# First k products of a linear-attention kernel: input transfers regrouped, PSUM copies on VectorE, product order changed, one operand sum placed later

## Chip, core and metric

The kernel runs on one NeuronCore of one Trainium2 chip. The metric is device time in microseconds, here called us. A core has TensorE (PE in the profile, with PEld for its weight loads), VectorE (DVE), ScalarE (ACT), GpSimd (POOL) and SyncE (SP). SP and ACT also issue transfers (DMAs) between HBM and SBUF, the on-chip memory; those two queues are SPq and ACTq in the profile. TensorE writes into PSUM, from which VectorE and ScalarE read.

## What is computed

Two linear-attention blocks, A and B, read the same x (2048 rows of 640) and are mixed by a gate:

```python
qkv = x @ wqkv                       # 640 x 1920, 32 heads of 20
phi = lambda t: where(t > 0, t + 1, exp(t)) + 1e-6
pq, pk = phi(q), phi(k)
kv  = einsum("bhsd,bhse->bhde", pk, v)
z   = einsum("bhsd->bhd", pk)
num = einsum("bhqd,bhde->bhqe", pq, kv)
den = einsum("bhqd,bhd->bhq", pq, z)[..., None] + 1e-6
block = (num / den).reshape(B, S, D) @ wo
g   = sigmoid((x * gate_w).sum(-1))
out = g * block_A + (1 - g) * block_B
```

All inputs and the output are bf16.

## The kernel before, in words

The 2048 rows are 16 chunks of 128 rows, the 640 columns are 5 blocks of 128. `xn` holds x by rows, `xT` holds it transposed (block c, then row), `wkA` and `wqA` hold A's key and query weights, block by block. The first 512 rows (chunks 0 to 3) come as rows and are transposed on TensorE; the other 1536 rows come transposed by 15 transposing DMAs (lines 157 to 161).

The first transfers, lines 147 to 156, in program order. On SP: x chunk 0, wkA block 0, the gate's weights `g5`, x chunks 2 and 3 together (320 KB), then wqA. On ACT: x chunk 1, wkA blocks 1, 2, and then 3 and 4 together (320 KB). The 15 transposing loads follow wqA on SP, and further on the row-wise loads of the rest of x (line 806), A's v and wo.

TensorE first runs seven warm-up products into a tile `warm` in PSUM slot 3 (lines 190 to 193). Then comes `k_first` (line 293). PSUM is a pool of four slots of two banks; a tile in a slot waits until the readers of the slot's former tile are through. `x_transpose(i, slot)` (line 230) transposes chunk i's five blocks into PSUM and copies them out to `xT`: VectorE takes blocks 0 and 1, ScalarE blocks 2 to 4. A product `k_mm(0, i, c, pt, hf)` (line 272) multiplies block c of chunk i with one half (`hf`, 320 columns) of wkA's block c. In A the second half has a 321st column, the gate's, which `gate_column` (line 205) brings there: a transpose of `g5` on TensorE into the PSUM tile it is given, and a copy into wkA by VectorE (line 208).

The order in `k_first` is written out by hand: transposes of chunks 0 and 1; chunk 0's first half for blocks 0 and 1; the gate column; chunk 1's first half for blocks 0 and 1; both second halves; block 2 for both chunks; transposes of chunks 2 and 3; and then 28 products with nothing else between (blocks 0 to 2 of chunk 2, six products; blocks 3 and 4 of chunks 0 to 2, twelve; all of chunk 3, ten). After each chunk's last product `k_done` (line 279) makes phi: an exponential on ScalarE (L248), one more for the gate (L282), and a clamp (L253) and a maximum (L262) on VectorE. The maximum reads the PSUM tile and ends its use.

A's first q products follow (L324, `q_block`), then k of chunks 4 to 7, more q, and k of chunks 8 to 15 (lines 801 to 818). `turn` gives the next of four slots; ahead of chunk 15 one slot is passed over (line 817), so that chunk 15 takes chunk 12's slot.

`sq_sum(k, r)` (line 347) are four sums and differences of pieces of `xT`, in halves r = 0 and 1, each 128 x 1024, all on VectorE. They become operands `SQ` of block B's q, which comes much later (`q_strassen`, from some 80 us on). The fourth of r = 0 stands behind chunk 8's phi (line 804). `q_pass` (line 773) makes the rest of A's q. After it come products of pk and x (`g_pass`, L454), on VectorE the third difference of pk (`k_sum(0, 3)`) and the four sums of r = 1 (line 827), and then `g_strassen` (L483). Inside it `rec_pass` makes the denominators (product L200, VectorE's product L612 and reciprocal L617) and `norm_spread` spreads them by products `exA` (L659), which read the reciprocals.

The engines run their own instructions in this order; nothing reorders the products. The whole span's order is by hand (`tc.manual_schedule()`).

Of the kernel before, what the change touches and what calls it, by code (L numbers as in the profile page):

```python
# [8 lines left out]
P = 128  # L9
FP32 = mybir.dt.float32  # L10
# [6 lines left out]
DT = D // P  # L17
# [15 lines left out]
def kernel(  # L33
# [11 lines left out]
    nc = tc.nc  # L45
# [28 lines left out]
    def ps_raw(name, slot=None):  # L74

        if slot is None:
            slot = turn[0]
            turn[0] = (slot + 1) % 4
        return pools["ps"].tile([P, 4 * HB], BF16, tag=f"ps{slot}", name=name)

    def ps(name, slot=None):

        return ps_raw(name, slot).bitcast(FP32).rearrange("p (b n) -> p b n", b=2)

    xT = persist.tile([P, DT, S], BF16, name="xT")
# [18 lines left out]
    hc, ic = ST // 2, 2 * P  # L104
# [36 lines left out]
    def load_x(eng, lo, hi):  # L141
        eng.dma_start(out=xn[:, lo:hi, :], in_=xb0[:, lo:hi, :])

    def load_wk(eng, lo, hi):
        eng.dma_start(out=wk[0][:, lo:hi, 0:D], in_=wq_dram[0][:, lo:hi, D:2 * D])
# [3 lines left out]
    load_wk(nc.sync, 0, 1)  # L149
    load_wk(nc.scalar, 1, 2)  # L150
    nc.sync.dma_start(out=g5[:], in_=gate_w.rearrange("(c p) -> c p", p=P))
    load_wk(nc.scalar, 2, 3)
    load_x(nc.sync, 2, 4)
    load_wk(nc.scalar, 3, DT)
    wq[0] = wpool.tile([P, DT, D], BF16, tag="wq", name="wqA")
    nc.sync.dma_start(out=wq[0][:], in_=wq_dram[0][:, :, 0:D])
    for n in range(1, NB):
        for c in range(DT):
            nc.sync.dma_start_transpose(
                out=xT[:, c, n * HB:(n + 1) * HB], in_=x2[n * HB:(n + 1) * HB, c * P:(c + 1) * P]  # L160
# [4 lines left out]
    for r in range(4):  # L165
# [3 lines left out]
        out=spread[:].rearrange("p (h t) -> p h t", t=TW), in_=I4[:, :, None].to_broadcast([P, H, TW])  # L169
    )  # L170
    nc.gpsimd.memset(maskE[:], 1.0)
    for sign, base in ((1, 0), (-1, Dh - 1)):
        nc.gpsimd.affine_select(
            out=maskE[:], in_=maskE[:], pattern=[[-sign * Dh, K6 // Dh], [0, Dh]],
# [3 lines left out]
    for r in range(4):  # L178
        rows = slice(32 * r, 32 * r + 32)
        for sign, base in ((1, 0), (-1, Dh - 1)):  # L180
            nc.gpsimd.affine_select(
                out=E4[rows], in_=E4[rows], pattern=[[sign, D]],
# [4 lines left out]
    ident32 = GT[0][:].rearrange("p c n -> p (c n)")[:, 0:2 * P].bitcast(FP32)  # L187
    make_identity(nc, ident32)

    warm = ps("warm", 3)  # L190
    one_l, one_r = [nc.const_aps.tensor(1.0, [P, n], BF16) for n in (P, HB)]
    for k in range(7):
        nc.tensor.matmul(warm[:, 0, :], lhsT=one_l, rhs=one_r, start=True, stop=True)
# [8 lines left out]
                    start=(c == 0), stop=(c == DT - 1), tile_position=(0, 32 * j),  # L202
                )

    def gate_column(pt):

        nc.tensor.transpose(out=pt[:, 2 * HB:2 * HB + DT], in_=g5[:], identity=ident[0:DT, 0:DT])
        nc.vector.tensor_copy(out=wk[0][:, :, D:D + 1], in_=pt[:, 2 * HB:2 * HB + DT, None])

# [20 lines left out]
    def x_transpose(i, slot):  # L230
        pt = ps_raw("xt", slot)
        for c in range(DT):
            nc.tensor.transpose(out=pt[:, c * P:(c + 1) * P], in_=xn[:, i, c * P:(c + 1) * P], identity=ident[:])
        src = pt[:, 0:D].rearrange("p (c n) -> p c n", c=DT)
        for copy, lo, hi in ((nc.vector.tensor_copy, 0, 2), (nc.scalar.copy, 2, DT)):
            copy(out=xT[:, lo:hi, i * P:(i + 1) * P], in_=src[:, lo:hi])  # L236
        return pt

    class Phi:

# [23 lines left out]
    def phi(dst, src, lifted=False, between=None):  # L264

        f = Phi(dst, src, lifted)
        f.clamp()
        if between is not None:
            between()
        f.top()  # L270

    def k_mm(b, i, c, pt, hf):
        n = HF + (b == 0 and hf == 1)
        nc.tensor.matmul(  # L274
            pt[:, hf, 0:n], lhsT=xT[:, c, i * P:(i + 1) * P], rhs=wk[b][:, c, hf * HF:hf * HF + n],
            start=(c == 0), stop=(c == DT - 1),
        )

    def k_done(b, i, pt):
        f = Phi(pk[:, i, :].rearrange("p (b n) -> p b n", b=2), pt[:, :, 0:HF])  # L280
        if b == 0:
            nc.scalar.activation(out=gl[:, i:i + 1], in_=pt[:, 1, HF:HF + 1], func=ACT.Exp)  # L282
        f.clamp()
        f.top()

    def k_chunk(b, i, slot=None):
        pt = ps(f"k{'AB'[b]}", slot)
        for hf in range(2):
            for c in range(DT):
                k_mm(b, i, c, pt, hf)  # L290
        k_done(b, i, pt)

    def k_first():

        pts = [ps("kA", (2 + i) % 4) for i in (0, 1)]

        def part(i, cs, hfs=(0, 1)):
            for c in cs:
                for hf in hfs:
                    k_mm(0, i, c, pts[i], hf)  # L300

        pt = [x_transpose(i, i) for i in range(2)]
        part(0, (0, 1), (0,))
        gate_column(pt[0])
        part(1, (0, 1), (0,))
        for i in range(2):
            part(i, (0, 1), (1,))
        for i in range(2):
            part(i, (2,))
        for i in (2, 3):  # L310
            x_transpose(i, i - 2)
        pts.append(ps("kA", 0))
        part(2, (0, 1, 2))
        for i in range(3):
            part(i, (3, 4))
            k_done(0, i, pts[i])
        k_chunk(0, 3, 1)
# [11 lines left out]
    def q_two(b, parts, pt):  # L329

        for u, (m, n) in enumerate(parts):
            for c in range(DT):
                q_mm(b, m, n, c, pt[:, u, :], c == 0, c == DT - 1)

    def q_unit(b, m, h, lifted=False, slot=None, between=None):

        pt = ps(f"q{'AB'[b]}", slot)
        q_two(b, [(m, 2 * h), (m, 2 * h + 1)], pt)
        phi(pqT[b][:, m, h * 2 * HB:(h + 1) * 2 * HB].rearrange("p (b n) -> p b n", b=2), pt, lifted, between)
# [7 lines left out]
    def sq_sum(k, r):  # L347

        lo, hi = [slice(n * HB, (n + 1) * HB) for n in (2 * r, 2 * r + 1)]
        x11, x12, x21, x22 = [xT[:, c:c + 2, rows] for rows in (lo, hi) for c in (0, 2)]  # L350
        a, b, op = {
            1: (x21, x22, ALU.add), 2: (SQ[:, 0, r], x11, ALU.subtract),
            3: (x11, x21, ALU.subtract), 4: (x12, SQ[:, 1, r], ALU.subtract),
        }[k]
        nc.vector.tensor_tensor(out=SQ[:, k - 1, r], in0=a, in1=b, op=op)
# [103 lines left out]
    def x_sum(k):  # L459

        x11, x21 = [xn[:, 0:hc, n:n + ic] for n in (0, ic)]
        x12, x22 = [xn[:, hc:ST, n:n + ic] for n in (0, ic)]
        a, b, op = {
            1: (x21, x22, ALU.add), 2: (SX[1], x11, ALU.subtract),
            3: (x11, x21, ALU.subtract), 4: (x12, SX[2], ALU.subtract),
        }[k]
        add_rows(SX[k], a, b, op)
# [72 lines left out]
    def z_rows(b, slot=None):  # L540

        pt = ps(f"z{'AB'[b]}", slot)
        for k in range(ST // 4):
            for hf in range(2):
                for j in range(4):
                    nc.tensor.matmul(
                        pt[32 * j:32 * j + 32, hf, 0:HF], lhsT=ones[:], rhs=pk[:, 4 * k + j, hf * HF:(hf + 1) * HF],
                        start=(k == 0), stop=(k == ST // 4 - 1), tile_position=(0, 32 * j),
                    )
        zr = work.tile([P, D], BF16, tag="zr", name="zr", bufs=1)  # L550
        nc.vector.tensor_tensor(
            out=zr[:].rearrange("p (b n) -> p b n", b=2), in0=pt[:, :, 0:HF],
            in1=E4[:].rearrange("p (b n) -> p b n", b=2), op=ALU.mult,
        )
        return zr
# [217 lines left out]
    def q_pass(units):  # L773

        units = list(units)
        q_unit(0, *units.pop(0))
        zr = z_rows(0)
        gate_spread()
        for k in range(2):
            x_sum(1 + k)  # L780
            q_unit(0, *units.pop(0), True)
        zsel = z_pass(0, zr)
        for k, (m, h) in enumerate(units):
            if k < 2:
                if k:
                    x_sum(3)
                else:
                    k_sum(0, 2)
            q_unit(0, m, h, True)
        return zsel  # L790

    with tc.manual_schedule():
        k_first()
        turn[0] = 2
        for n in range(2):
            for i in range(CB if n else 0, CB * 2 * n):
                k_chunk(0, i)
            for m in (0, 2):
                q_block(0, m, n, (lambda k: lambda: sq_sum(k, 0))(1 + m // 2) if n else None)
        q_unit(0, DT - 1, 0, True, None, lambda: sq_sum(3, 0))  # L800
        for i in range(hc, ST - 2):
            k_chunk(0, i)
            if i == hc:
                sq_sum(4, 0)
    for n in range(1, NB):
        nc.sync.dma_start(
            out=xn[:, n * CB:(n + 1) * CB, :], in_=x2[n * HB:(n + 1) * HB, :].rearrange("(q p) d -> p q d", p=P)
# [4 lines left out]
    def bank(pool, name, n=1):  # L812
        return pool.tile([P, HB] if n == 1 else [P, n, HB], FP32, tag=name, name=name)

    with tc.manual_schedule():
# [114 lines left out]
        part = [slice(n * RB, (n + 1) * RB) for n in range(4)]  # L930
# [23 lines left out]
        with late_pool("single") as single:  # L954
# [6 lines left out]
            pts = [bank(single, f"s4{hf}")[:, 0:HF] for hf in range(2)]  # L961
# [21 lines left out]
        for i in range(1, half):  # L983
            p, after = pairs[i], pairs[i + 1] if i + 1 < half else None
# [53 lines left out]
```

## Time and profile before

| | us |
|---|---|
| time, median of 3 runs | 190.37 (190.33 to 191.26) |
| the profiled execution | 190.57 |
| its span | 188.9 |
| TensorE busy in the span | 182.9 |
| VectorE busy | 154.6 |
| ScalarE busy | 88.5 |

The profile shows one execution, and its times count from the span's start. A line of the timeline gives start, duration, engine, line of the kernel, operation, output and inputs, a count where instructions are merged, and in brackets how long the engine was idle just before and what released it. In a list of waits stand the waiting instruction, what it waited for, and us in total, times and the longest. Ends of products are modelled, so that a product's duration (299 ns for 320 columns) is longer than the distance from one start to the next. TensorE's granted clock is 1.00 in the whole span.

### The profile page before, as it was taken

Reading aid. Unit: us, or ns where it says so; the run is one execution under the profiler, and the core shown is the slowest. Engines: PE = TensorE matmul, PEld = TensorE weight load, DVE = VectorE, ACT = ScalarE, POOL = GpSimd, SP = SyncE. Lnnn points to the kernel's source line nnn. Section 1 sums busy time; section 2 is a strip of 40 time slices with the busy share of each in tenths; the row PEclk is TensorE's granted clock in tenths of the full one; section 3 lists DMA queues with packets and bytes.
Section 4 is the critical chain, followed back from the end, with each engine's and each line's share of the span. In section 5 each row is a group of like instructions: output and inputs, shape, how many; then the busy total and the mean of one; then the engine's idle time right before and its main releaser. Section 6 shows DMA issues by size and latency. Waiting matters only on the chain.

```text
span 188.9 us, 3632 instructions
## 1 busy us (share of the span) xinstructions
PE 182.9 (97%) x1447; PEld 122.4 (65%) x1456; DVE 154.6 (82%) x265; ACT 88.5 (47%) x153; POOL 9.1 (5%) x25
## 2 busy tenths in 40 slices
PE   8799999999999999999999999999999999999994
PEld 3465656755567677666666665667677876777772
DVE  1258868889999999998898987999997989787644
ACT  2364669544873251563959595761621611111120
POOL 8910000000000000000000000000000000000000
PEclk9999999999999999999999999999999999999999
DMA  6995559925441000004100000045800002311122
GB/s 169 305 177 88 106 106 377 310 51 168 107 119 58 0 3 0 0 0 134 43 0 2 3 0 0 2 138 181 209 0 0 3 0 73 122 68 68 70 95 70
DMA packets 19593, 16.18 MB, mean 86 GB/s; under 512 B 8920, under 2 KB 19320, under 8 KB 19576
## 3 DMA queue, kind: packets, MB, share of 16 engines
q1 hardware_dynamic: 18584, 14.96, 28.1%
q10 hardware_dynamic: 992, 0.98, 1.7%
q8 instruction: 11, 0.18, 0.4%
q14 instruction: 6, 0.05, 0.1%
HBM read 10.52 MB, written 3.46 MB: 74 GB/s over the span
## 4 chain that ended last, share of the span: by engine, by line
PE 90%; DVE 3%; DMA 3%; ACT 1%; issue 1%; ACTq 0%; DVEq 0%
PE gs L483 16%; PE qA L324 11%; PE kB L274 11%; PE kA L274 11%; PE q L378 7%; PE ox L683 6%; PE oy L683 5%; PE oz L683 5%; DMA wkA<-in_A_wqkv_dram 3%; PE ow L683 3%; PE gB L454 2%; PE gA L454 2%; PE qB L324 1%; PE q L324 1%; DVE osb L688 1%; PE mA L898 1%
## 5 line engine op out<-in xcount | busy, mean ns | idle before, releaser
L274 PEld LDWEIGHTS <-xT 128*128 128x128 bf16 x320 | 31.0, 97 | 16.9 <-issue 2.0
L253 DVE TENSOR_SCALAR e<-e 128x640 bf16<-128x640 bf16 (+2 forms) x56 | 19.3, 345 | 8.3 <-ACT e L248 8.0
L274 PE MATMUL kA<-wkA,xT 128*128 128x320 bf16 (+1 forms) x160 | 23.0, 299 | 1.6 <-ACT xT L236 0.6
L274 PE MATMUL kB<-wkB,xT 128*128 128x320 bf16 x160 | 24.2, 299 | 0.0
L324 PE MATMUL qA<-xT,wqA 128*128 128x512 bf16 x96 | 22.4, 379 | 0.2
L324 PEld LDWEIGHTS <-wqA 128*128 128x128 bf16 x100 | 11.7, 118 | 9.2 <-issue 0.3
L248 ACT ACTIVATE e<-kB 128x640 bf16<-128x640 f32 x16 | 11.3, 708 | 9.0 <-PE kB L274 8.9
L483 PEld LDWEIGHTS <-xn 128*128 128x128 bf16 x128 | 12.2, 98 | 5.2 <-issue 0.5
L262 DVE SCALAR_TENSOR_TENSOR pk<-kA,e 128x640 bf16<-128x640 f32 x16 | 13.2, 825 | 2.6 <-ACT gl L282 0.6
L248 ACT ACTIVATE e<-kA 128x640 bf16<-128x640 f32 x16 | 11.2, 706 | 7.8 <-PE kA L274 7.8
L262 DVE SCALAR_TENSOR_TENSOR pk<-kB,e 128x640 bf16<-128x640 f32 x16 | 13.2, 824 | 1.5
L248 ACT ACTIVATE e<-qA 128x1024 bf16<-128x1024 f32 x10 | 10.2, 1024 | 8.3 <-PE qA L324 7.9
L727 ACT COPY u<-ox 128x320 f32<-128x320 f32 x8 | 3.4, 425 | 21.6 <-PE ox L683 21.6
L248 ACT ACTIVATE e<-q 128x512 bf16<-128x512 f32 x18 | 10.8, 597 | 5.4 <-PE q L378 3.8
L683 PEld LDWEIGHTS <-xT 128*128 128x128 bf16 x85 | 8.0, 98 | 3.1 <-DVE xT L622 0.2
L683 PEld LDWEIGHTS <-pqTA 128*128 128x128 bf16 x85 | 7.9, 98 | 2.9 <-issue 0.2
L683 PEld LDWEIGHTS <-pqTB 128*128 128x128 bf16 x80 | 7.8, 98 | 3.0
L378 PE MATMUL q<-xT,wqB 128*128 128x512 bf16 x32 | 9.5, 379 | 0.0
L483 PE MATMUL gs<-pk,xn 128*128 128x320 bf16 x64 | 9.5, 299 | 0.0
L688 DVE TENSOR_TENSOR osb<-oz,u 128x320 bf16<-128x320 f32 (+1 forms) x18 | 8.0, 453 | 1.5 <-PE oz L683 0.7
L711 ACT COPY p1s<-ox 128x320 f32<-128x320 f32 x8 | 3.4, 426 | 10.3 <-PE ox L683 10.3
L454 PEld LDWEIGHTS <-xn 128*128 128x128 bf16 x64 | 6.3, 98 | 3.0 <-issue 0.4
(151 smaller groups left out, 319.3 us busy)
## 6 DMA issues: line engine op xcount, KB each, us to landing
out_dram<-osb SPq DMA_DIRECT2D x14, 160.0 KB, 1.8
xn<-in_A_x_dram SPq DMA_DIRECT2D x3, 640.0 KB, 6.2
wqA<-in_A_wqkv_dram SPq DMA_DIRECT2D x1, 800.0 KB, 6.4
wvA<-in_A_wqkv_dram SPq DMA_DIRECT2D x1, 800.0 KB
wkB<-in_B_wqkv_dram SPq DMA_DIRECT2D x1, 800.0 KB, 4.7
wqB<-in_B_wqkv_dram SPq DMA_DIRECT2D x1, 800.0 KB, 4.7
wvB<-in_B_wqkv_dram SPq DMA_DIRECT2D x1, 800.0 KB
MA<-m_rows SPq DMA_DIRECT2D x1, 800.0 KB, 4.7
```

Of the source, the lines that this page charges most:

```text
L248: nc.scalar.activation(out=to, in_=part, func=ACT.Exp)
L253: nc.vector.tensor_scalar(self.e, self.e, 1.0, EPS, op0=ALU.min, op1=ALU.add)
L262: nc.vector.scalar_tensor_tensor(out=dst, in0=src, scalar=1.0 + EPS, in1=e, op0=ALU.add, op1=ALU.max)
L274: nc.tensor.matmul(pt[:, hf, 0:n], lhsT=xT[:, c, i * P:(i + 1) * P], rhs=wk[b][:, c, hf * HF:hf * HF + n], start=(c == 0), stop=(c == DT - 1),
L324: nc.tensor.matmul(dst, lhsT=mixed(wq[b][:, c, :], m), rhs=xT[:, c, n * HB:(n + 1) * HB], start=first, stop=last,)
L378: nc.tensor.matmul(dst, lhsT=left(c), rhs=right(c), start=first and k == 0, stop=k == len(cs) - 1, skip_group_check=not first,)
L454: nc.tensor.matmul(pt[:, hf, 0:HF], lhsT=xn[:, i, c * P:(c + 1) * P], rhs=pk[:, i, hf * HF:(hf + 1) * HF], start=(i == 0), stop=(i == ST - 1),
L483: nc.tensor.matmul(pt[:, n, 0:HF], lhsT=left[:, i, n * P:(n + 1) * P], rhs=right[:, i, :], start=(first and i == 0), stop=(i == hc - 1), s ...
L683: nc.tensor.matmul(dst, lhsT=left[:, c, r0:r0 + P], rhs=right[:, c, :], start=(first and c == 0), stop=(c == DT - 1), skip_group_check=not ...
L688: nc.vector.tensor_tensor(out=dst, in0=acc, in1=sb, op=ALU.add)
L711: nc.scalar.copy(out=self.p1s[:], in_=self.at("x"))
L727: nc.scalar.copy(out=self.u2[:], in_=self.at("x"))
```

## The change

Four things change.

The transfers: x's chunks 2 and 3 (the third and fourth) come in two transfers of 160 KB on ACT's queue, and wkA's block 2 and blocks 3 and 4 go to SP's queue. The copies: `x_transpose` copies all five blocks by VectorE, in two instructions. The order in `k_first`: the gate column's transpose goes into the warm-up's tile, right behind chunk 0's first half; chunk 0's second half follows, then all of chunk 1's blocks 0 and 1, the transposes of chunk 2, block 2 of both chunks, the transposes of chunk 3, and the same 28 products as before. The sum: `sq_sum(4, 0)` moves from behind chunk 8 to the end of `q_pass`, behind A's last q.

```diff
@@ transfers @@
-    load_wk(nc.scalar, 2, 3)
-    load_x(nc.sync, 2, 4)
-    load_wk(nc.scalar, 3, DT)
+    load_x(nc.scalar, 2, 3)
+    load_wk(nc.sync, 2, 3)
+    load_x(nc.scalar, 3, 4)
+    load_wk(nc.sync, 3, DT)
@@ the warm-up's tile and the gate column @@
-    warm = ps("warm", 3)
+    warm_raw = ps_raw("warm", 3)
+    warm = warm_raw.bitcast(FP32).rearrange("p (b n) -> p b n", b=2)
...
-    def gate_column(pt):
+    def gate_column():
+        pt = warm_raw
@@ x_transpose @@
-        for copy, lo, hi in ((nc.vector.tensor_copy, 0, 2), (nc.scalar.copy, 2, DT)):
-            copy(out=xT[:, lo:hi, i * P:(i + 1) * P], in_=src[:, lo:hi])
-        return pt
+        for lo, hi in ((0, 2), (2, DT)):
+            nc.vector.tensor_copy(out=xT[:, lo:hi, i * P:(i + 1) * P], in_=src[:, lo:hi])
@@ k_first @@
-        pts = [ps("kA", (2 + i) % 4) for i in (0, 1)]
+        pts = []
...
-        pt = [x_transpose(i, i) for i in range(2)]
+        x_transpose(0, 0)
+        x_transpose(1, 1)
+        pts.append(ps("kA", 2))
         part(0, (0, 1), (0,))
-        gate_column(pt[0])
-        part(1, (0, 1), (0,))
-        for i in range(2):
-            part(i, (0, 1), (1,))
+        gate_column()
+        pts.append(ps("kA", 3))
+        part(0, (0, 1), (1,))
+        part(1, (0, 1))
+        x_transpose(2, 0)
         for i in range(2):
             part(i, (2,))
-        for i in (2, 3):
-            x_transpose(i, i - 2)
+        x_transpose(3, 1)
         pts.append(ps("kA", 0))
         part(2, (0, 1, 2))
@@ q_pass, its end @@
             q_unit(0, m, h, True)
+        sq_sum(4, 0)
         return zsel
@@ k of chunks 8 to 13 @@
             k_chunk(0, i)
-            if i == hc:
-                sq_sum(4, 0)
```

## The prediction

> **What bounds the kernel now.** I read the page first, then the waits of TensorE over the whole span, then the timeline of the first 20 us.
>
> ```profile
> span 188.9 us, 3632 instructions
> ...
> PE 182.9 (97%) x1447; PEld 122.4 (65%) x1456; DVE 154.6 (82%) x265; ACT 88.5 (47%) x153; POOL 9.1 (5%) x25
> ```
>
> ```profile
> PE kA L274 <- ACT xT L236: 0.6, 1, 0.6
> PE kA L274 <- DMA wkA<-in_A_wqkv_dram: 0.6, 1, 0.6
> PE kA L274 <- DVE pk L262: 0.3, 1, 0.3
> ```
>
> TensorE is busy for 97% of the span, and beyond its start it waits three times for other engines: twice in the first k (0.6 us each) and once for VectorE (0.3 us). The change reaches all three and takes no product away. What it can win is those waits, and smaller gaps between instructions around them.
>
> ```profile
> 3.97 0.98 PE L233 MATMUL xt<-ident,xn 128*128 128x128 bf16 x10
> 4.12 0.39 SPq L156 DMA_DIRECT2D wqA<-in_A_wqkv_dram  x1
> ...
> 4.71 0.57 DVE L236 COPY xT<-xt 128x256 bf16<-128x256 bf16 x2 [3.23 <-PE xt L233]
> ...
> 5.06 0.45 PE L274 MATMUL kA<-wkA,xT 128*128 128x320 bf16 x2
> ...
> 5.57 0.16 PE L207 MATMUL xt<-ident,g 5*128 5x5 bf16 x1
> ...
> 5.66 1.04 PE L274 MATMUL kA<-wkA,xT 128*128 128x320 bf16 x6
> 5.76 0.18 DVE L208 COPY wkA<-xt 128x5 bf16<-128x5 bf16 x1 [0.48 <-PE xt L207]
> 7.29 0.71 PE L274 MATMUL kA<-wkA,xT 128*128 128x320 bf16 x4 [0.58 <-DMA wkA<-in_A_wqkv_dram]
> ...
> 7.84 0.72 PE L233 MATMUL xt<-ident,xn 128*128 128x128 bf16 x10
> ...
> 9.17 4.00 PE L274 MATMUL kA<-wkA,xT 128*128 128x320 bf16 x28 [0.61 <-ACT xT L236]
> ...
> 13.00 4.48 PE L324 MATMUL qA<-xT,wqA 128*128 128x512 bf16 x19
> ```
>
> From 5.06 to 9.17 TensorE does 12 products, 10 transposes and the gate column's transpose, some 2.4 us of work in 4.11 us. From 9.17 on it streams 28 products. So the yardstick for the start is when those 28 begin. Everything behind keeps its order on TensorE, so that an earlier start carries through unless something is late in its turn.
>
> **The first k, step by step.** The two transposes and the first two products keep their inputs, so VectorE begins its copies at 4.71 again. What a copy costs stands in the groups by shape of the first 14 us (mean ns behind the busy time).
>
> ```profile
> L236 ACT COPY xT<-xt 128x384 bf16<-128x384 bf16 x4 | 1.7, 482 | 3.8 <-DVE xT L236 3.8
> L233 PE MATMUL xt<-ident,xn 128*128 128x128 bf16 x20 | 1.7, 242 | 0.0
> ...
> L236 DVE COPY xT<-xt 128x256 bf16<-128x256 bf16 x4 | 1.1, 292 | 5.6 <-PE xt L233 5.6
> ```
>
> New are VectorE's copies of three blocks (384 elements). With the gate copy above (0.18 us for 5 elements) its own sizes give (292-180)/(256-5) = 0.45 ns an element, hence 292+128x0.45 = 350 ns. The bounds are 292, its smaller copy, and 482, ScalarE's copy of that size; I take 350, being the same engine. [...]
>
> The gate copy now stands behind four copies on VectorE: 4.71+0.29+0.35+0.29+0.35+0.18 = 6.17. The second half's products of chunk 0 wait for it, since they read wkA's gate column; before, TensorE had two products between, and they ran from 5.66. That is a stall of some 0.6 us put in, ahead of everything that is queued on TensorE, although chunk 1's first-half products behind them need no gate column. The gate's transpose goes into the warm-up's tile and no longer waits for ScalarE's copies out of the old one; chunk 1's accumulator takes that tile's slot, and its wait for the gate copy is the same wait. Both are worth nothing beside 6.17. Behind it nothing waits any longer if the transfers are there: six products at 4.00/28 = 0.143 end at 7.03; five transposes, starting (0.72-0.24)/9 = 0.053 apart (0.24 is one's own run), end at 7.30; four products take 7.84-7.29 = 0.55, to 7.85; five transposes end at 8.12. Chunk 2's copies run under these: its last transpose is through at 7.30+0.19, copies take 0.29+0.35, and 0.06 for two handovers give 8.19. The 28 products begin at 8.19 instead of 9.17: 0.98 us won, if no transfer is late.
>
> How long the transfers take stands in three views: the chain of waits (start, duration), the DMA issues (KB each, us from issue to landing) and the windows, whose last figure is GB/s and the third from the end TensorE's granted clock.
>
> ```profile
> 1.73 5.52 DMA wkA<-in_A_wqkv_dram
> ```
>
> ```profile
> wqA<-in_A_wqkv_dram SPq DMA_DIRECT2D x1, 800.0 KB, 6.4
> ...
> xn<-in_A_x_dram SPq DMA_DIRECT2D x1, 320.0 KB, 5.6
> wkA<-in_A_wqkv_dram ACTq DMA_DIRECT2D x1, 320.0 KB, 6.3
> ```
>
> ```profile
> 5.06:7.29 2.23, 1.58 (x10) 0.80 (x10) 0.40 (x2) 0.84 (x2) 2.03 (x4) 1.00 0.81 253
> 7.29:9.17 1.88, 1.27 (x15) 1.01 (x14) 0.57 (x2) 0.53 (x2) 1.72 (x4) 1.00 1.04 376
> ```
>
> x's third chunk takes the third place on ACT's queue, where wkA's third block landed at 1.73+5.52 = 7.25. It competes with 160 KB on SP instead of 320, so it may land earlier: by 5.06 the first products run, so both first chunks and wkA's first two blocks are there; the next two transfers are 0.33 MB, 1.3 us at 253 GB/s, to 6.4. TensorE wants it at 7.03. Between "in time" (8.19) and 7.25 (7.29+0.27+0.19+0.64+0.06 = 8.45) I take the middle: 8.32, a gain of 0.85. wkA's third block, now where x's 320 KB landed at 2.12+5.6 = 7.7, is half as large and may be there at 6.4 by the same sum; wanted at 7.30. x's fourth chunk comes where wkA's 320 KB landed by 2.2+6.3 = 8.5, also half as large: 0.16 MB more, 0.65 us at 253, about 7.0; wanted at 7.85. At 8.5, the worst, the 28 products begin at 8.5+0.04+0.27 = 8.81, and 0.36 is left of the gain. The upper bound is 292 ns copies: 8.07, a gain of 1.10.
>
> SP's queue, by its own waits:
>
> ```profile
> SPq L156 <- DMA xn<-in_A_x_dram: 1.6, 1, 1.6
> ```
>
> wkA's last two blocks move behind on SP. The kernel's ninth load (wqA at line 156, behind four on each queue) waited on SP for an x chunk to land, to 4.12; the ninth is now the last blocks', and I put the wait there. Queued behind it on SP are wqA (4.12+0.43 = 4.55) and all 15 transposing loads, each some 0.43 us later. The last blocks are wanted after six of the 28, at 8.32+0.86 = 9.18. From below: from 5.06 on, two x chunks, wkA's third block and these are 0.82 MB; 0.56 MB of it moves by 7.29 at 253 GB/s and 0.26 MB at 376 takes 0.7 us: 8.0. From above they land like the 800 KB issued at 4.12: 10.54. They are 320 KB, so I take 8.3 and no stall. wqA lands at 4.55+6.4 = 10.95, wanted at 13.00-0.85 = 12.15.
>
> The transposing loads, with the DMA issues around 9.2 us (landing) and the timeline:
>
> ```profile
> xT<-in_A_x_dram SPq DMA_TRANSPOSE x2, 3.8
> ...
> 10.54 1.26 SPq L159 DMA_TRANSPOSE xT<-in_A_x_dram  x1
> ...
> 17.32 0.30 PE L274 MATMUL kA<-wkA,xT 128*128 128x320 bf16 x1
> ```
>
> ```profile
> 25.53 1.68 SPq L806 DMA_DIRECT2D xn<-in_A_x_dram  x3
> ...
> 47.11 1.22 DVE L622 TENSOR_TENSOR S<-xn 128x2048 bf16<-128x2048 bf16 x1
> ```
>
> The fifth transposing load (issued at 10.54) lands some 3.8 us on, the fourth's price: 14.3, then 14.8; chunk 4 wants it at 17.32-0.85 = 16.47. Cover 1.6 us; without it, at wqA's 6.4, it would land at 17.4 and 0.9 would be lost. x's later blocks, behind them all, are issued at 25.5 and first used at 47.1: over 15 us of cover. ScalarE loses four copies and gains no wait. Its exponentials start when chunk 0's products end, as before.
>
> **The fourth sum.** It leaves VectorE's order at chunk 8 and comes back after A's q. The timelines of VectorE and TensorE:
>
> ```profile
> 33.31 0.68 DVE L355 TENSOR_TENSOR SQ<-xT,SQ 128x1024 bf16<-128x1024 bf16 x1
> 33.91 0.32 DVE L253 TENSOR_SCALAR e<-e 128x640 bf16<-128x640 bf16 x1
> ...
> 38.36 0.82 DVE L262 SCALAR_TENSOR_TENSOR pk<-kA,e 128x640 bf16<-128x640 f32 x1
> ...
> 60.02 0.69 DVE L355 TENSOR_TENSOR SQ<-xT,SQ 128x1024 bf16<-128x1024 bf16 x1
> 61.13 0.42 DVE L612 SCALAR_TENSOR_TENSOR d<-denA,ge 128x256 f32<-128x256 f32 x1 [0.42 <-PE denA L200]
> ...
> 63.65 1.75 DVE L617 RECIPROCAL rT<-d 128x256 bf16<-128x256 f32 x1
> ```
>
> ```profile
> 39.23 1.52 PE L274 MATMUL kA<-wkA,xT 128*128 128x320 bf16 x10 [0.29 <-DVE pk L262]
> ...
> 65.46 0.40 PE L659 MATMUL exA<-rT,spread 32*128 32x256 bf16 x8
> ```
>
> The last k chunk's accumulator comes free when VectorE ends chunk 12 at 39.18. Without 0.60 us of sum ahead of it (33.31 to the next start at 33.91) that is 38.6, before TensorE asks at 38.94: all 0.29 won. It is put ahead of the third difference of pk and the second round of four sums, and delays what follows on VectorE: the denominators' product at 61.13. Cover there is 0.42 us of idle time. VectorE is 0.29 earlier with TensorE and 0.60 later: 0.60-0.42 = 0.18 late for it, and its reciprocal ends at 65.40-0.29+0.18 = 65.29. TensorE reads it in the second half of exA, at about 65.46+0.20-0.29 = 65.37. So it just fits; without cover (VectorE not earlier by 0.29) the price is about 0.3 to 0.4. The term is 0.29, between -0.1 and 0.29.
>
> Sum: 0.85+0.29 = 1.14. The profiled execution took 190.57 us (span 188.9, 1.7 around it), 0.2 over the median of 190.37. The span becomes 187.8, such a run 189.4, the median 189.2.
>
> **Rivals.**
>
> (B) Transfers set the pace: x's chunks land where third and fourth transfers on ACT's queue landed. For it: two transfers instead of one, and TensorE wants them within 0.9 us. Against: half the bytes in each place. Gain 0.36+0.29 = 0.65, 189.7. [...]
>
> (C) The sum's 0.29 is given back at exA. For it: in the stretch ahead of the new place VectorE is busy 11.94 of 12.59 us (row below), so it has little to give. Against: the 0.42 of idle at 61.13. 190.37-0.85 = 189.5; with the full price 189.6.
>
> ```profile
> 40.60:53.19 12.59, 12.46 (x89) 6.82 (x89) 11.94 (x19) 8.06 (x10) 0.00 (x0) 1.00 0.38 108
> ```
>
> (D) Slower: the last two blocks, issued by SP only at 4.12, land late. Chunks 0 to 2 cannot end without them. It decides from 9.18 on; at 10.54 the products that began at 9.17+0.86 = 10.03 begin at 10.58, 0.55 lost against 0.29 won: 190.6. For it: wqA's row; against: it is 800 KB.
>
> (E) A cost that no row shows, such as a lower granted clock after the new stall (1.00 in both windows above, in spite of 1.2 us of waits): 191.4 or more.
>
> **How the numbers follow.** Forecast 0.62, B 0.20, C 0.06, D 0.08, E 0.04. I call 0.5% (0.95 us) what a measurement tells from no change. Faster: 0.56 of the forecast's and 0.04 of B's, 0.60. Slower: E and half of D (landing past 11.3), 0.08. The same: 0.32. The range runs from 188.8 (all upper bounds, 1.39, and the spread of the runs) to 190.4 (B, C and the milder D inside); the forecast's own is 188.9 to 189.5.
>
> **What would show it.** Right: the 28 products beginning near 8.3; one wait before the six products, for the gate copy at 6.2; no wait for pk near 38; exA without a wait. Wrong: a wait for wkA behind 9, for xn over 0.3 us, for rT, or copies of 384 elements near 480 ns, which put the start at 8.4.

## The result, and the profile after

| | before | changed |
|---|---|---|
| time, median (us) | 190.37 (190.10 to 191.26, 7 runs) | 189.65 (188.84 to 189.96, 7 runs) |
| ratio, 95% interval | | 0.9946 (0.9922 to 0.997) |
| the profiled execution, its span (us) | 190.57, 188.9 | 189.96, 188.2 |

The change is faster: 0.72 us by the medians, 1.0 by the ratio, which is one of means, and the interval reaches from 0.3% to 0.8%. Six of the runs of e3 below (192.82 to 195.05 us) and the only run of e4 had a granted clock of 0.98 to 0.99, where all others had 0.998 or more, and no ratio counts them. The profiled execution was the slowest of the seven; its trace shows two places where it lost time, but the other six were not traced. First its page and its waits (us in total, times, longest).

```profile
span 188.2 us, 3633 instructions
...
PE 182.4 (97%) x1447; PEld 122.1 (65%) x1456; DVE 155.7 (83%) x269; ACT 86.8 (46%) x149; POOL 9.1 (5%) x25
```

```profile
PE qA L328 <- DVE pk L264: 0.9, 1, 0.9
...
PE kA L276 <- DVE wkA L211: 0.3, 1, 0.3
```

The three waits of before (a wkA block, ScalarE's copy, VectorE's pk) are gone. Two others are there: 0.3 us for the gate copy, and 0.9 us in front of A's first q. Lines have moved by a few: copies are L239, the gate copy L211, products of k L276, of q L328. The timeline of the changed kernel, TensorE, VectorE and SP's queue:

```profile
3.89 0.39 SPq L145 DMA_DIRECT2D wkA<-in_A_wqkv_dram  x1
4.32 0.47 SPq L157 DMA_DIRECT2D wqA<-in_A_wqkv_dram  x1
4.38 1.02 DVE L239 COPY xT<-xt 128x256 bf16<-128x256 bf16 x4 [2.90 <-PE xt L236]
...
5.32 0.18 DVE L211 COPY wkA<-warm 128x5 bf16<-128x5 bf16 x1
5.55 0.98 PE L276 MATMUL kA<-wkA,xT 128*128 128x321 bf16 x6 [0.27 <-DVE wkA L211]
...
7.48 4.00 PE L276 MATMUL kA<-wkA,xT 128*128 128x320 bf16 x28
...
12.41 0.59 PEld L328 LDWEIGHTS <-wqA 128*128 128x128 bf16 x4 [1.27 <-DMA wqA<-in_A_wqkv_dram]
...
28.71 11.06 PE L276 MATMUL kA<-wkA,xT 128*128 128x320 bf16 x80
39.62 2.32 PE L328 MATMUL qA<-xT,wqA 128*128 128x512 bf16 x9
...
60.24 0.42 DVE L616 SCALAR_TENSOR_TENSOR d<-denA,ge 128x256 f32<-128x256 f32 x1
...
64.48 0.40 PE L663 MATMUL exA<-rT,spread 32*128 32x256 bf16 x8
...
100.38 0.69 DVE L259 TENSOR_TENSOR pqTB<-pqTB,e 128x1024 bf16<-128x1024 bf16 x1 [0.48 <-ACT pqTB L252]
...
184.44 0.86 PE L687 MATMUL oz<-MB,xT 128*128 128x160 bf16 x10
```

The 28 products begin at 7.48 instead of 9.17, a lead of 1.69 us. At q the lead is only 0.59 (12.41 against 13.00). The row of TensorE's weight load names what q waited for: wqA's transfer. The list of waits names VectorE's pk for the same wait, because that instruction happened to end at 12.41 too (in e5, below, q begins ahead of that instruction, so it does not need it). The DMA issues (KB each, us from issue to landing) carry the rest of it:

```profile
wqA<-in_A_wqkv_dram SPq DMA_DIRECT2D x1, 800.0 KB, 8.0
xn<-in_A_x_dram ACTq DMA_DIRECT2D x3, 160.0 KB, 3.1
wkA<-in_A_wqkv_dram SPq DMA_DIRECT2D x2, 160.0 KB, 3.7
wkA<-in_A_wqkv_dram SPq DMA_DIRECT2D x1, 320.0 KB, 3.6
```

wqA, issued at 4.32, landed 8.0 us later, at 12.3; before it was 4.12 and 6.4, at 10.5. What is split and moved around it came early: no product waited for x or wkA, and the last two blocks were there at 3.89+3.6 = 7.5.

Behind q, the row of 80 products has no wait for pk any more, and the lead grows from 0.59 to 0.98 (39.62 against 40.60). It is 0.98 again at exA (64.48 against 65.46). Then it falls: the last row here is one of the last products, at 184.44, and the kernel before has it at 185.19:

```profile
35.97 0.82 DVE L262 SCALAR_TENSOR_TENSOR pk<-kA,e 128x640 bf16<-128x640 f32 x1 [0.55 <-ACT gl L282]
...
101.03 0.69 DVE L257 TENSOR_TENSOR pqTB<-pqTB,e 128x1024 bf16<-128x1024 bf16 x1
...
104.80 0.38 PE L378 MATMUL q<-SQ,MB 128*128 128x512 bf16 x1
...
185.19 0.85 PE L683 MATMUL oz<-MB,xT 128*128 128x160 bf16 x10
```

That leaves 0.75. The 0.23 between went at 104 us: VectorE stood idle for 0.48 us ahead of its instruction at 100.38, where the same instruction of the kernel before (101.03) has no such wait, and TensorE's product that comes at 104.80 before comes at 104.06, a lead of 0.74. The chain of work that ended last (start, duration) runs through VectorE there, and in the kernel before it stays on TensorE:

```profile
103.31 0.70 DVE q L400
104.01 0.04 issue
104.06 0.38 PE q L382
```

### The profile page after: what moved, and what is told of

The parts are those of the page before. It is cut to its first block, busy times and chain, and to the rows that moved or that the text cites. A ratio compares the mean times of both kernels' runs of the same rounds, so it can differ in the third digit from the quotient of the medians.

```text
span 188.2 us, 3633 instructions
## 1 busy us (share of the span) xinstructions
PE 182.4 (97%) x1447; PEld 122.1 (65%) x1456; DVE 155.7 (83%) x269; ACT 86.8 (46%) x149; POOL 9.1 (5%) x25
## 4 chain that ended last, share of the span: by engine, by line
PE 93%; DVE 4%; ACT 1%; issue 1%; DVEq 0%; ACTq 0%
PE gs L487 16%; PE kA L276 12%; PE qA L328 12%; PE kB L276 10%; PE q L382 7%; PE ox L687 6%; PE oy L687 5%; PE oz L687 5%; PE ow L687 3%; PE gB L458 2%; PE gA L458 2%; PE warm L195 2%; PE qB L328 1%; PE q L328 1%; DVE osb L692 1%; PE mA L901 1%
## 5 line engine op out<-in xcount | busy, mean ns | idle before, releaser
L276 PEld LDWEIGHTS <-xT 128*128 128x128 bf16 x320 | 30.9, 97 | 15.1 <-issue 0.5
L276 PE MATMUL kB<-wkB,xT 128*128 128x320 bf16 x160 | 24.2, 299 | 0.0
L328 PE MATMUL qA<-xT,wqA 128*128 128x512 bf16 x96 | 22.4, 380 | 1.2 <-DVE pk L264 0.9
L276 PE MATMUL kA<-wkA,xT 128*128 128x320 bf16 (+1 forms) x160 | 22.8, 299 | 0.4 <-DVE wkA L211 0.3
L328 PEld LDWEIGHTS <-wqA 128*128 128x128 bf16 x100 | 11.6, 118 | 10.4 <-DMA wqA<-in_A_wqkv_dram 1.3
L250 ACT ACTIVATE e<-kB 128x640 bf16<-128x640 f32 x16 | 11.3, 708 | 9.0 <-PE kB L276 7.4
L250 ACT ACTIVATE e<-qA 128x1024 bf16<-128x1024 f32 x10 | 10.2, 1023 | 9.4 <-PE qA L328 9.0
L715 ACT COPY p1s<-ox 128x320 f32<-128x320 f32 x8 | 3.4, 425 | 10.3 <-PE ox L687 10.3
```

The costliest lines, as they stand in the source:

```text
L250: nc.scalar.activation(out=to, in_=part, func=ACT.Exp)
L276: nc.tensor.matmul(pt[:, hf, 0:n], lhsT=xT[:, c, i * P:(i + 1) * P], rhs=wk[b][:, c, hf * HF:hf * HF + n], start=(c == 0), stop=(c == DT - 1),
L328: nc.tensor.matmul(dst, lhsT=mixed(wq[b][:, c, :], m), rhs=xT[:, c, n * HB:(n + 1) * HB], start=first, stop=last,)
L715: nc.scalar.copy(out=self.p1s[:], in_=self.at("x"))
```

## The experiments

Every group of runs had the kernel before beside it on the same chip, and its ratio is to that. The columns "28" and "q" are the starts of the 28 products and of A's first q in the profiled execution, "wqA" its issue and its landing, and "behind q" the time from q's start to that late row at 184 to 185 us, a measure of all that follows the start.

| run | ratio (95%) | 28 | q | wqA | behind q |
|---|---|---|---|---|---|
| before | 1 | 9.17 | 13.00 | 4.12, 10.5 | 172.19 |
| changed | 0.9946 (0.9922 to 0.997) | 7.48 | 12.41 | 4.32, 12.3 | 172.03 |
| e5, the change again | 0.9939 (0.9925 to 0.9954) | 7.78 | 11.64 | 4.46, 11.6 | 172.05 |
| e1, the sum alone | 0.9972 (0.996 to 0.9983) | 9.22 | 13.05 | 3.92, 10.5 | 171.73 |
| e2, all but the sum | 0.9934 (0.9918 to 0.9951) | 8.02 | 11.86 | 4.49, 10.5 | 172.00 |
| e8, old transfers | 0.9986 (0.9973 to 0.9999) | 9.25 | 13.09 | 3.67, 10.7 | 171.98 |
| e9, new transfers alone | 0.9969 (0.9952 to 0.9985) | 8.70 | 12.53 | 4.33, 11.8 | 172.19 |
| e10, joined transfers alone | 0.9986 (0.9962 to 1.0011) | 8.22 | 12.06 | 3.71, 10.0 | 172.18 |
| e6, ScalarE copies | 0.9939 (0.9917 to 0.9961) | 7.67 | 12.93 | 4.32, 12.9 | 171.77 |
| e7, x joined | 0.991 (0.9894 to 0.9926) | 7.99 | 11.82 | 3.63, 10.3 | 171.74 |
| e12, x joined, again | 0.9933 (0.9914 to 0.9952) | 8.28 | 12.12 | 3.86, 10.2 | 171.74 |
| e11, wqA issued by ACT | 0.9934 (0.9907 to 0.9962) | 7.93 | 11.77 | 3.81, 11.3 | 171.97 |
| e3, last blocks by ACT | 1.0005 (0.9982 to 1.0027) | 7.41 | 12.45 | 3.60, 9.5 | 171.96 |

**The sum alone, and all but the sum.** e1 is the kernel before with the sum moved:

```diff
             q_unit(0, m, h, True)
+        sq_sum(4, 0)
...
-            if i == hc:
-                sq_sum(4, 0)
```

> The kernel before with the fourth sum alone moved behind A's last q. My theory: TensorE's 0.29 us wait for VectorE's pk before the last k chunk goes, with some 0.1 us of restart behind it, and nothing is given back: 0.3 to 0.45 us faster. Rival: VectorE is late for the denominators, exA waits for the reciprocals, and the time is within 0.1 us of the kernel before.

e2 is the changed kernel with the sum back behind chunk 8:

```diff
-        sq_sum(4, 0)
...
+            if i == hc:
+                sq_sum(4, 0)
```

> The changed kernel with the fourth sum back behind chunk 8. My theory: what is won here is the start alone, 0.4 to 0.7 us against the kernel before, the wait for wqA included, and a 0.29 us wait for pk stands before the last k chunk. Rival: the start brings nothing once wqA's lateness is counted (within 0.2 us of the kernel before), and all of the gain is the sum's.

Measured: e1 took 190.16 us against 190.75, 0.53 us by the ratio, a little over what was expected. The wait for pk is gone, and 0.46 us are gone behind q. e2 missed its own theory and its rival: 189.50 us, 1.26 us by the ratio, more than expected and as much as the whole change. Its timeline of TensorE and VectorE around chunk 12:

```profile
28.10 11.10 PE L276 MATMUL kA<-wkA,xT 128*128 128x320 bf16 x80
39.03 2.32 PE L328 MATMUL qA<-xT,wqA 128*128 128x512 bf16 x10
...
32.17 0.68 DVE L359 TENSOR_TENSOR SQ<-xT,SQ 128x1024 bf16<-128x1024 bf16 x1
```

The sum stands in its old place (32.17), and still the 80 products run without a wait, from 28.10 to q at 39.03: 10.93 us, as in the changed kernel (28.71 to 39.62, 10.91) and 0.42 less than before (29.25 to 40.60, 11.35). What is missing is the pause of 0.55 us that the kernel before has on VectorE at 35.97. So the wait for pk had two parts, the sum's 0.60 and a pause of 0.55, and taking either away was enough. e1 does not tell them apart, since that pause is gone in it as well as the sum. The changed kernel, e5 and e7 do: there the sum is moved, a pause of 0.54 to 0.56 is on VectorE (33.65, 32.91, 32.99), and TensorE has no wait for pk.

**The change again.** e5 is the changed kernel itself, once more.

> The changed kernel once more. Theory (the start's gain is partly taken back by wqA, whose slowest DMA engine ends at a different time in each execution): 0.7 to 1.6 us faster than the kernel before, the first q waiting between 0 and 0.9 us for wqA in the profiled execution. Rival (the parts do not add, whatever wqA does): the first q starts without a wait and the time is still only 0.7 to 1.0 us below the kernel before.

189.28 us (189.17 to 189.59) against 190.53: 1.16 us by the ratio. Its timeline of TensorE and VectorE shows the difference to the first profile:

```profile
7.78 4.00 PE L276 MATMUL kA<-wkA,xT 128*128 128x320 bf16 x28
11.64 2.57 PE L328 MATMUL qA<-xT,wqA 128*128 128x512 bf16 x10
...
11.76 0.82 DVE L264 SCALAR_TENSOR_TENSOR pk<-kA,e 128x640 bf16<-128x640 f32 x1
```

wqA landed at 4.46+7.1 = 11.6, just as the 28 products and the rest of chunk 3 were through, and q followed without a listed wait, ahead of chunk 1's pk on VectorE. The 28 began 0.30 later than in the first profile, yet q 0.77 earlier. The time is inside what the theory allowed (0.7 to 1.6) and above what the rival did (0.7 to 1.0).

**Which part makes the start: order, or transfers?** e8 is the changed kernel with the transfers of before, e9 the kernel before with the new transfers:

```diff
@@ e8, against the changed kernel @@
-    load_x(nc.scalar, 2, 3)
-    load_wk(nc.sync, 2, 3)
-    load_x(nc.scalar, 3, 4)
-    load_wk(nc.sync, 3, DT)
+    load_wk(nc.scalar, 2, 3)
+    load_x(nc.sync, 2, 4)
+    load_wk(nc.scalar, 3, DT)
```

> The new order and copies with the transfers of the kernel before. Theory (the start's gain is the transfers'): TensorE's six products are done by 7.0, the transposes of chunk 2 wait for x to 7.5 or later, the 28 products begin at 8.6 or later, and the gain against the kernel before is 0.5 to 0.9 us, of it 0.4 the sum's. Rival (order and copies alone bring it): the 28 products begin before 8.3.

> The kernel before with the change's transfers alone: its own order of products, ScalarE's copies and its own place of the fourth sum. Theory 1 (transfers and order together make the gain at the start): the wait for wkA's third block at 7.29 goes, so its four products end at about 7.2 and the ten transposes at 8.0, but the wait of 0.6 for ScalarE's copy stays behind them, and the 28 products begin at about 8.6 instead of 9.2. With A's pk wait of 0.3 kept, the time is about 0.6 us (0.3%) below the kernel before, ratio 0.997. Theory 2 (the transfers are all of it): the 28 products begin at 8.0 as they do with the whole start, and the ratio is that of the start alone, 0.993. Theory 3 (each needs the other): ratio 0.999 to 1.001, as the new order with the old transfers gained next to nothing at the start.

e8 gained 0.27 us, less than the sum alone and less than the 0.5 to 0.9 of its theory: with the old transfers the new order and the copies won nothing at the start, and behind q it has a pause of 0.47 us on VectorE at 101.00 that e1 does not have. e9 gained 0.59 us, close to what its first theory said, though the wait for wkA's third block, which the theory took away, is still 0.51. TensorE of e8, and then of e9:

```profile
8.13 0.45 PE L235 MATMUL xt<-ident,xn 128*128 128x128 bf16 x5 [0.83 <-DMA xn<-in_A_x_dram]
...
9.25 4.00 PE L275 MATMUL kA<-wkA,xT 128*128 128x320 bf16 x28
```

```profile
6.82 0.71 PE L275 MATMUL kA<-wkA,xT 128*128 128x320 bf16 x4 [0.51 <-DMA wkA<-in_A_wqkv_dram]
...
8.70 4.00 PE L275 MATMUL kA<-wkA,xT 128*128 128x320 bf16 x28 [0.61 <-ACT xT L237]
```

In e8 the transposes of chunk 2 wait 0.83 us for the 320 KB of x, and what the order saves is spent there. In e9 the transposes come early enough, but the old order leaves nothing to do while the copies of chunk 2 run: the 0.61 stays in front of the 28 products. Each alone meets the other's wait: the order can take its part only when the transfers are in time. e10 is e9 with the two x chunks in one transfer:

```diff
-    load_wk(nc.scalar, 2, 3)
-    load_x(nc.sync, 2, 4)
-    load_wk(nc.scalar, 3, DT)
+    load_x(nc.scalar, 2, 4)
+    load_wk(nc.sync, 2, 3)
+    load_wk(nc.sync, 3, DT)
```

> The kernel before with the transfers of the joined version alone (x's chunks 3 and 4 in one transfer on ScalarE's queue, wkA's third and last blocks on SP's): order of products, copies and the fourth sum as before. By theory 1 (transfers and order together) the 28 products begin at about 8.6 as with the split transfers, and the time is 0.6 to 0.9 us below the kernel before, the upper value if A's q finds wqA earlier: ratio 0.995 to 0.997. By theory 2 (transfers are all) it is what the joined version gained without the sum's 0.5, ratio 0.994, with the 28 products at 8.0. If it is equal to the run with split transfers, the joining is worth nothing without the new order.

Its 28 products begin at 8.22, better than forecast and 0.48 ahead of e9, since wkA's third block is there without a wait, and q at 12.06, 0.94 before its place in the kernel before. Yet the six runs lie between 189.62 and 191.13, and the interval holds 1. The profiled execution is the 189.62; what delayed the others was not recorded.

**Who copies.** e6 is the changed kernel with blocks 2 to 4 copied by ScalarE:

```diff
-        for lo, hi in ((0, 2), (2, DT)):
-            nc.vector.tensor_copy(out=xT[:, lo:hi, i * P:(i + 1) * P], in_=src[:, lo:hi])
+        for copy, lo, hi in ((nc.vector.tensor_copy, 0, 2), (nc.scalar.copy, 2, DT)):
+            copy(out=xT[:, lo:hi, i * P:(i + 1) * P], in_=src[:, lo:hi])
```

> The changed kernel with ScalarE copying blocks 2 to 4 out of PSUM again. Theory (the gate copy behind four VectorE copies costs TensorE its 0.27 us wait): the gate copy ends some 0.4 us earlier, the wait goes, and the 28 products begin 0.2 to 0.3 us earlier after the first transposes than in the changed kernel. Rival: ScalarE's copies are late for the products instead (block 2 of chunks 0 and 1, chunk 2's slot), and the 28 products begin no earlier.

e6 has the same ratio as the change. In its timeline the gate copy has no VectorE copies of three blocks ahead of it, and TensorE still waits as long for it, against the theory:

```profile
5.52 0.98 PE L276 MATMUL kA<-wkA,xT 128*128 128x321 bf16 x6 [0.27 <-DVE wkA L211]
...
7.17 0.44 PE L236 MATMUL xt<-ident,xn 128*128 128x128 bf16 x5
7.67 4.00 PE L276 MATMUL kA<-wkA,xT 128*128 128x320 bf16 x28
...
12.93 1.27 PE L328 MATMUL qA<-xT,wqA 128*128 128x512 bf16 x4 [1.26 <-DMA wqA<-in_A_wqkv_dram]
```

So 0.27 us is the way from the gate's transpose through its copy, and the four copies in front of it on VectorE add nothing. VectorE's copies bring something else, which the rival named: with ScalarE's the 28 products begin 0.50 us behind the start of the five transposes ahead of them, where the changed kernel has 7.48-7.20 = 0.28. This profile has the late wqA again, at its worst: 8.6 us from issue to landing, and the execution (190.20) was the slowest of its six, as with the first profile of the change.

**Why wqA comes late.** In e4 the transposing loads, which follow wqA on SP, are held back until it has landed: a store of one of its rows stands ahead of them, and the row-wise load of x's second quarter goes between.

```diff
+        nc.sync.dma_start(out=m_rows[0:1, 0:D], in_=wq[0][0:1, 0, 0:D])
         for n in range(1, NB):
...
                 nc.sync.dma_start_transpose(
```

> The changed kernel with a small store of a row of wqA ahead of the transposing loads on SP, which makes them wait until wqA has landed; x's rows 512 to 1023 are loaded in between. Theory 2 (transposing loads hold up wqA's tail): wqA lands by 10.0 and the first q does not wait for it; the transposing loads come later, and chunk 4 waits for them instead, so that the whole is slower. Theory 1 (late issue and queue): wqA lands at 11.5 or later all the same.

e4 has one run, 195.16 us, of which 3.1 us are TensorE's waits for transposed x, which now comes late. wqA took 7.3 us from its issue at 4.50 with no transposing load under way, and landed at 11.8, as the first theory had it. So wqA comes late without them too. But 640 KB of x, issued at 5.01 behind it on the same queue, were under way in their place; whether any load behind wqA holds it up stays open. In e3 the last two wkA blocks go back to ACT, behind x's chunks, so that SP has wqA next:

```diff
-    load_wk(nc.sync, 3, DT)
+    load_wk(nc.scalar, 3, DT)
```

> The changed kernel with wkA's blocks 3 and 4 issued by ACT, behind x's fourth chunk, so that SP has only wkA's third block ahead of wqA. Theory 1 (wqA is late because SP issues it last, behind 320 KB more on the same queue): it lands by 10.6 as in the kernel before, the first q waits 0.1 us or less, and the kernel is 0.5 to 0.9 us faster than the changed one. Theory 2 (wqA is late because the transposing loads behind it on SP get onto the DMA engines before its last packets are through): it lands after 11.5 again, and the time is within 0.3 us of the changed kernel.

wqA landed at 3.60+5.9 = 9.5, and q had no wait for it. But now the blocks themselves were late:

```profile
7.41 0.99 PE L276 MATMUL kA<-wkA,xT 128*128 128x320 bf16 x6
9.44 3.17 PE L276 MATMUL kA<-wkA,xT 128*128 128x320 bf16 x22 [1.05 <-DMA wkA<-in_A_wqkv_dram]
```

With 800 KB of wqA moving beside them they took 5.6 us, and TensorE waited 1.05 us after the first six of the 28. So e3's first theory was right about wqA and missed the time. The six runs that its ratio counts scatter from 189.79 to 191.35; what makes them differ is left open. e11 has ACT issue wqA, behind x's chunks, and leaves the blocks on SP:

```diff
-    nc.sync.dma_start(out=wq[0][:], in_=wq_dram[0][:, :, 0:D])
+    nc.scalar.dma_start(out=wq[0][:], in_=wq_dram[0][:, :, 0:D])
```

> The changed kernel with wqA issued by ScalarE behind x's fourth chunk instead of by SP behind wkA's last blocks; the transposing loads then come first on SP behind these blocks. Theory 1 (wqA comes late because it is issued late, behind SP's wait for a landing and behind the last blocks): wqA is issued at about 3.5 instead of 4.3 to 4.5 and lands by 10.9, A's q has no wait for it, and the time is 0.3 to 0.8 us below the changed kernel: ratio to the kernel before 0.990 to 0.992. Theory 2 (its slowest engine decides, whoever issues it, and the transposing loads compete with it): it lands at 11.5 to 13 again, with the ratio of the changed kernel (0.994) or above.

wqA was issued at 3.81 and landed at 11.3, 0.4 later than its first theory said; q began at 11.77 with no wait. The median is 189.03 (188.76 to 190.62) against 190.62. The ratio's interval, 0.9907 to 0.9962, holds both theories' values. e7 leaves the queues as the change has them and joins x's third and fourth chunks, one transfer fewer ahead of wqA:

```diff
-    load_x(nc.scalar, 2, 3)
+    load_x(nc.scalar, 2, 4)
     load_wk(nc.sync, 2, 3)
-    load_x(nc.scalar, 3, 4)
     load_wk(nc.sync, 3, DT)
```

> The changed kernel with x's third and fourth chunks in one transfer of 320 KB on ACT. Theory (the split is what brings the third chunk early): both land at 6.5 to 7.7, the transposes of chunk 2 wait 0.3 to 1.2 us, and the 28 products begin after 8.0. Rival (the bytes ahead decide, not the split): the transfer lands by 6.5 and TensorE waits 0.2 us or less.

> The version with x's chunks 3 and 4 joined, once more and on whatever chip comes. Theory 1 (one load fewer ahead of wqA takes the wait for a landing off wkA's last blocks, so wqA is issued near 3.65 and is there before A's q asks for it): the ratio to the kernel before is 0.990 to 0.993 again, wqA lands by 11 and A's q has no wait. Theory 2 (the first run of it drew a good landing of wqA by chance): wqA lands at 11.5 or later in this profile, and the ratio is that of the changed kernel, 0.994 to 0.995.

e7 took 188.89 us (188.46 to 189.01), all five runs below all six of the change on the same chip (189.17 to 189.59). Its start came as its theory said, at the near end: a wait of 0.3 for x, and the 28 products at 7.99. e12 took 189.29 against 190.43, a ratio that the change's interval holds too. Of the two theories stated for e12 the first had the mechanism: wqA landed at 10.2 and q had no wait. But the ratio it gave, 0.990 to 0.993, was just missed. The timelines of e7, TensorE and then SP's queue, show the trade:

```profile
6.87 0.45 PE L235 MATMUL xt<-ident,xn 128*128 128x128 bf16 x5 [0.30 <-DMA xn<-in_A_x_dram]
...
7.99 4.00 PE L275 MATMUL kA<-wkA,xT 128*128 128x320 bf16 x28
11.82 2.54 PE L327 MATMUL qA<-xT,wqA 128*128 128x512 bf16 x10
...
2.12 0.82 SPq L145 DMA_DIRECT2D wkA<-in_A_wqkv_dram  x2
3.63 0.38 SPq L156 DMA_DIRECT2D wqA<-in_A_wqkv_dram  x1
```

The last blocks are issued at once behind the third (two in 0.82 us), the wait for a landing falls on wqA (0.7 us in e7; in the change it is 1.4 and falls on the last blocks), and it is issued 0.5 to 0.8 us earlier than in the change. The larger x transfer costs 0.3 us of waiting (0.2 in e12), and the 28 products begin at 7.99 and 8.28. In the profiles q starts at 11.82 and 12.12, not earlier than the change's 11.64 at its best, but ahead of the 12.41 of the first profile and the 12.93 of e6. The other part stands in the last column: 0.3 us less behind q than in the change, since the pause at 100 us does not show there:

```profile
99.41 0.69 DVE L258 TENSOR_TENSOR pqTB<-pqTB,e 128x1024 bf16<-128x1024 bf16 x1 [0.15 <-ACT pqTB L251]
```

So this version beats the kernel before in both runs and the changed kernel in the one where they stood side by side. How much it gains over the change (between 0.1% and 0.3% by the ratios) is not settled.

## Why the prediction was right

The sign was right, and for the reason given: an earlier start and a wait for pk less. 189.65 lies inside the range (188.8 to 190.4), 0.45 above the forecast of 189.2 and 0.15 above the forecast's own range; it is nearer to rival B's 189.7, though not by B's mechanism. The second group of runs (e5, 189.28) hit the forecast. Whether the gain is over 0.5% one comparison leaves open (0.3% to 0.8%); e5's interval lies above it but for its edge (0.46% to 0.75%). The steps, one by one:

- *The start, 0.85.* It was under-sized: the 28 products came 1.15 to 1.69 us earlier (8.02 in e2, 7.78 in e5, 7.48 in the first profile; forecast 8.32). Three terms were off. VectorE began at 4.38 where 4.71 was carried over: that start varies by execution (4.37 in e1, 4.62 in e5, 4.66 in e2), and in the kernel before it made no difference, because the next transfer was waited for anyway (0.58 us for wkA; in e1 0.96 for x, and its 28 products came at 9.22). The gate copy came 1.12 us behind the first copy and not 1.46. And x and wkA were in time, where the middle between in time and late was taken. In-time sum less the first two: 8.19-0.33-0.34 = 7.52, and 7.48 was measured.
- *Copies of 384 elements at 350 ns.* This was right by the groups by shape (below): 348. The error was to lay four durations end to end. The four took 1.02 us together, where their durations add up to 1.28: one starts before the row of the one ahead has ended. The stall for the gate copy was 0.27 instead of 0.6: the copy began at 5.32, just as the gate's transpose (5.11+0.17) ended, and e6 shows that the copies ahead had no part in it.

```profile
L239 DVE COPY xT<-xt 128x384 bf16<-128x384 bf16 x4 | 1.4, 348 | 0.0
L239 DVE COPY xT<-xt 128x256 bf16<-128x256 bf16 x4 | 1.2, 290 | 4.5 <-PE xt L236 4.5
```

- *The last two blocks, 8.3, no stall.* This was right, and they came early: 7.5, wanted at 7.48+0.86 = 8.34. Rival D falls. e3 shows how near it lies: issued elsewhere, the same blocks cost 1.05 us. Rival E falls too: the granted clock of the profiled execution is 1.00.
- *wqA at 10.95, wanted at 12.15, no wait.* This step failed in the profiled execution. It was issued as forecast (4.32 against 4.55) but took 8.0 us and not 6.4, and the earlier products wanted it at 12.41-0.93 = 11.48. With x split and wqA behind all of wkA on SP it took 6.0 to 8.6 us in the profiles of the change, e2, e4, e5, e6 and e9, against 6.3 to 7.0 in those of before, e1, e7, e8, e10 and e12; with x split too, e3 has 5.9 and e11, where ACT issues it, 7.5. The 6.4 was one draw, used as a constant, and the range for this step was left out. What is lost here is the part of the start's lead above what wqA allows, 0 to 1.3 us by execution, and it cancels the under-sized start. That the total came out nearer than its parts is luck.
- *The sum, 0.29.* The wait went as forecast, and 0.44 us with it (11.35 less 10.91). But it was not the sum's alone: e2 has it in the old place without the wait, because a pause on VectorE is not there. With the rest of the change the sum was worth nothing that these runs could tell (e2 0.9934, e5 0.9939).
- *exA just fits.* This was right, as close as forecast: the second reciprocal ends at 64.51 and the products of exA that read it begin at 64.60, 0.09 later, where 0.08 was worked out. VectorE's product at 60.24 has no idle time left ahead of it. Rival C, that the gain is given back at exA, falls. 0.23 to 0.26 is given back at 104 us instead, on a pause that no step had.
- *Rival B, the transfers set the pace.* It did not come as stated, since none was late; but e8 (0.83 us of waiting for x) and e9 show that they were what set it before. What joining two of these transfers of 160 KB is worth the runs do not settle: in the old order the 28 products began 0.48 us earlier with x joined (e10 against e9), in the new order joined x was waited for, 0.2 to 0.3 us, and yet the kernel was no slower and on one chip 0.3% faster (e7).

## What to carry to other kernels

When a start is bound by transfers and by order at once, try both together: either alone can measure as nothing (in e8 the 28 products begin at 9.25, before at 9.17) because it runs into the other's wait. When a big load is issued later or behind more bytes, take its time from issue to landing from several profiles and carry its spread as a range (5.9 to 8.6 us for the 800 KB here); its slack shrinks by as much as the work in front of it gets faster. And before pricing a wait on an engine, look whether all that delays it belongs to the instruction that is to be moved (here 0.60 us did, and a pause of 0.55 did not).

## What was not expected of the hardware

**One load's time varies by 2.6 us between executions with the same transfers.** wqA is 800 KB in every kernel, and took 6.0 us in e2 and 8.6 in e6, whose transfers are the same. The windows of the changed kernel and then of the kernel before, last figure GB/s:

```profile
9.50:10.00 0.50, 0.50 (x6) 0.34 (x5) 0.21 (x1) 0.50 (x3) 0.50 (x1) 1.00 4.53 106
10.00:11.00 1.00, 1.00 (x9) 0.72 (x8) 0.85 (x2) 1.00 (x4) 0.37 (x2) 1.00 0.66 57
11.00:12.00 1.00, 0.48 (x4) 0.10 (x2) 0.87 (x3) 0.63 (x3) 0.00 (x0) 1.00 0.19 35
```

```profile
9.50:10.00 0.50, 0.50 (x6) 0.34 (x5) 0.00 (x0) 0.00 (x1) 0.50 (x1) 1.00 1.63 237
10.00:11.00 1.00, 1.00 (x10) 0.71 (x8) 0.00 (x0) 0.26 (x1) 0.37 (x2) 1.00 1.08 197
11.00:12.00 1.00, 1.00 (x9) 0.72 (x8) 0.38 (x2) 1.00 (x4) 0.00 (x0) 1.00 1.27 252
```

From 9.5 to 12 the changed kernel moves 106, 57 and 35 GB/s where the kernel before moves 197 to 252, and yet wqA is not there, nor do the loads behind it get on (the first transposing load lands at 13.1, in the kernel before at 11.1). The single packets in its trace tell more. wqA is 640 packets of 1280 bytes. All but 77 of them end by 9.5, and the last at 12.03 (in e2, where wqA took 6.0 us, all but 18 end by 9.5). Meanwhile 26 packets of 256 and 4 bytes, started between 9.0 and 10.4, take 1.9 to 3.2 us and end together at 12.21 to 12.24, and the 16 landings of wqA come between 12.30 and 12.36. So most of the load had moved in time, and its landing came with its last packets. In e4, with nothing transposing behind, the 16 landings lie between 9.0 and 11.85: the first came 2.8 us before the last, and the first weight load of q, at 11.89, came behind the last (in the changed kernel 12.41, behind 12.36). In the other traces at least 15 of the 16 landings lie within 0.2 us (0.6 in e11). Why the last packets lag is not settled; e4 shows a lag without transposing loads, but with 640 KB of x behind wqA instead.

**VectorE pauses at the same count of its records in most kernels.** Counting all of VectorE's records in the trace, those that only wait for a semaphore too, the 64th has 0.54 to 0.56 us of idle time in the timelines of the kernel before and of ten of the thirteen others, though it comes at another time and stands elsewhere in the work in each kind of kernel: chunk 10's pk at 35.97 before, and in the changed kernel this one, one chunk earlier:

```profile
33.65 0.82 DVE L264 SCALAR_TENSOR_TENSOR pk<-kA,e 128x640 bf16<-128x640 f32 x1 [0.55 <-DVE e L255]
```

The three without it are e1, e2 and e6. In the eleven the 64th record is always a maximum that makes pk, right behind a record that waits for a semaphore; in e1 and e6 it is a clamp, in e2 the waiting record itself, so the count alone does not make the pause. The instruction at 100.38 in the changed kernel, with 0.48 us ahead of it, is the 192nd record, 128 further on; it is that in e2, e3, e4, e5, e8 and e11 too, with 0.46 to 0.48 us. In the other seven kernels the same instruction is not the 192nd, and at most 0.15 us are ahead of it. The price stands in the last column above: with the sum moved it is 171.96 to 172.05 where this pause is and 171.73 to 171.77 where it is not. So it looks as if a few instructions more or fewer early on an engine can move a pause to where it hurts, or to where it does not, far behind the edit. What the pause is no run here tells.
